# Filling up small constant tiles so that matmul operands in SBUF begin at multiples of 128 bytes

## The chip, the cores and the metric

The kernel runs on one core of one Trainium2 chip. The metric is the device time of one execution in microseconds (us). A lower number is better. The kernel of before was timed three times. Besides that there is one execution taken by the hardware profiler; the page and all rows below come from it.

## What is computed

Two batches of eight heads of attention (768 positions, head size 64), in which a query may only look at keys that belong to the same of 16 clusters, are followed by two layers that each expand 512 features to 2048 and go back to 512, without any routing. Everything is float32.

```python
# attention, per batch and head; q, k, v are 768 x 64
q_assign = argmax(normalised(q) @ normalised(centroids).T)     # 16 clusters
k_assign = argmax(normalised(k) @ normalised(centroids).T)
scores = where(q_assign == k_assign, q @ k.T / 8, -1e9)
x = softmax(scores) @ v                    # heads side by side: 1536 x 512
# layer 1                                  # layer 2
h = x @ w_in          # 512 -> 2048        h = x @ w_in
g = h * cos(h)                             g = h if h >= 1, 0 if h <= -1, else (h+1)**2/4
x = g @ w_out         # 2048 -> 512        out = g @ w_out
```

## The kernel before

**Precision.** TensorE multiplies in the type `F32R` (reduced float32). The kernel gets full precision by splitting a number into a high part (rounded to `F32R`) and a low part (the rest), and by adding products of the parts. So most operands exist twice: `th`/`tl` (transposed q and k), `phi`/`plo` (transposed probabilities), `xh`/`xl` (input of a layer), `gh`/`gl` (its hidden values), and the two halves of each weight tile `w_n`.

**Attention.** There are 8 pairs of heads (`prep_pair` prepares each) and 192 slots (`run_slot`), 24 for a pair. In one slot TensorE does three transposes of 128 columns (`p_transpose`, L527: the probabilities `p` are the operand that is loaded into the array, the identity `ident` is the one that is streamed), two score matmuls of 384 columns (`scores`, L475 and L478: one `st` tile is loaded, another is streamed) and two matmuls of 384 columns with v (`p_v`, L545 and L546: `vv` is loaded, `phi` and then `plo` are streamed). That is 192 x 4 = 768 matmuls of 384 columns in all. In some slots the preparation of the next pair comes on top (transposes L329, cluster products L367 and L368 that stream `cn`, transposes L449). ScalarE copies `phi` out of PSUM (L530) and takes the exponential (L493). VectorE makes `plo` (L535) and the row maximum `nm` (L484). GpSimd makes the parts of q, k, v and x.

**Layers.** For each of 2 layers, 4 quarters of the hidden features and 3 blocks of 512 tokens, `hidden` runs 48 matmuls of 512 columns and then `output` of the group before runs 48. Both go through `mm3` (L699 to L701). In `hidden` a weight is loaded and `xh`, `xl`, `xh` are streamed. In `output` of layer 1 a weight is loaded and `gh`, `gl`, `gh` are streamed; in layer 2 `gh` or `gl` is loaded and a weight is streamed. So 24 groups of 48 (1,152 matmuls) write `h` and 24 groups (1,152) write `y`. In the profile's rows a matmul's name gives its result first, then the streamed operand, then the loaded one, except that the identity of a transpose stands first as the streamed one.

**Where the tiles lie.** Each pool puts its tiles behind each other in a partition of SBUF and rounds a tile's size up to a multiple of 32 bytes. `cpool` holds the constants. In it a few tiles of 4 to 16 bytes take 32 bytes each, and what lies behind them begins at odd multiples of 32 bytes. In the attention's pool `css` (20 bytes) and the two `mx` tiles (96 bytes) do the same. Every piece of an operand that a matmul streams begins a multiple of 128 bytes behind the start of its tile; so the start of the tile decides.

What sets the order of work is the slot loop and, for most of the attention, a fixed order by hand; the change touches neither.

Of the kernel before, what the change touches and what calls it, by code (L numbers as in the profile page):

```python
# [8 lines left out]
F32 = mybir.dt.float32  # L9
F32R = mybir.dt.float32r  # L10
I32 = mybir.dt.int32
# [7 lines left out]
P = 128  # L19
# [13 lines left out]
def attention_moe_moe(  # L33
# [18 lines left out]
    nc = tc.nc  # L52
# [16 lines left out]
    cpool = ctx.enter_context(tc.tile_pool(name="cpool", bufs=1))  # L69
# [10 lines left out]
        nc.gpsimd.memset(ohbias[32 * r:32 * r + 32], 0.0 if is_q else -BIG)  # L80

    own = cpool.tile([P, 2, 2], F32, name="own")
    row = cpool.tile([P, 1], I32, name="row")
    nc.gpsimd.iota(row, pattern=[[0, 1]], base=0, channel_multiplier=1)
    nc.vector.tensor_scalar(row, row, C, None, ALU.bitwise_and)
    for h in range(2):
        half = BIG / C if h else -BIG / C
# [3 lines left out]
    idle = cpool.tile([P, 512], BF16, name="idle")  # L91
    nc.vector.memset(idle, 0.0)

    xh = cpool.tile([P, NPAIR, NT], F32R, name="xh")
    xl = cpool.tile([P, NPAIR, NT], F32R, name="xl")
    cn = cpool.tile([P, NPAIR, 2, 2, C], F32R, name="cn")
# [93 lines left out]
    with ExitStack() as actx:  # L190
        ap = actx.enter_context(tc.tile_pool(name="apool", bufs=1))
# [19 lines left out]
        def ins(x):  # L211
            return x.ins if hasattr(x, "ins") else x
# [20 lines left out]
        def centroid_setup(ct):  # L233
            sq = ct[:, 1]
            nc.vector.tensor_tensor(sq, ct[:, 0], ct[:, 0], ALU.mult)
            ss = ap.tile([P, 5], F32, tag="css", name="css")
            nc.vector.tensor_reduce(ss[:, 0:1], sq, AX.X, ALU.add)
            y = ss[:, 1:2]
            sq = nc.scalar.activation(y, ss[:, 0:1], AF.Sqrt)
            with tc.issue_after(ins(sq)):  # L240

                nc.scalar.activation(ss[:, 4:5], desc[:, 0:1], AF.Exp, scale=0.0)
            for _ in range(2):
                nc.vector.tensor_scalar(y, y, 1e-30, None, ALU.max)
                nc.vector.reciprocal(ss[:, 2:3], y)
                nc.vector.scalar_tensor_tensor(
                    ss[:, 3:4], ss[:, 0:1], ss[:, 2:3], y, ALU.mult, ALU.add)
                nc.vector.tensor_scalar(y, ss[:, 3:4], 0.5, None, ALU.mult)
            nc.vector.tensor_scalar(ss[:, 2:3], y, 1e-6, None, ALU.add)
            nc.vector.reciprocal(ss[:, 3:4], ss[:, 2:3])  # L250
            cd = ap.tile([P, HS], F32, tag="xt1", bufs=2, name="cd")[:, :P].rearrange(
                "p (r d) -> p r d", r=2)
            for r in range(2):
                nc.vector.tensor_scalar(cd[:, r], ct[:, 0], ss[:, 3:4], None, ALU.mult)
            nc.vector.memset(cn.bitcast(F32), 0.0)
            return cd
# [19 lines left out]
        def prep_pair(i):  # L276
# [95 lines left out]
                        yield  # L372

            G = NJ * 4
            mx = ap.tile([P, G], F32, tag="mx", bufs=2, name=f"mx{i}")
            eq = ap.tile([P, G, C], F32, tag="eq", bufs=1, name=f"eq{i}")
            if i == 0:
                run_idle(NIDLE[2], ins(mm))
# [217 lines left out]
        idle_o = ps_o.tile([P, 512], F32, tag="o", name="idle_o")  # L596
        run_idle(NIDLE[0])
        cd = centroid_setup(ct)
        for _ in prep_pair(0):
            next_slot()  # L600
# [9 lines left out]
        def run_slot(slot):  # L610
            g = slot + LEAD
            if slot in prep_at:
                preps.append(prep_pair(prep_at[slot]))
            if 0 <= slot < NSLOT:
                p_transpose(slot // NJ, slot % NJ)
            if 0 <= g < NSLOT:
                scores(g // 2, g % 2)
            for u, kt in pv_slots.get(slot, ()):
                p_v(u, kt)
            if slot % 2 == 0:  # L620
                for s in (slot - 1, slot):
                    if 0 <= s < NSLOT:
                        p_lo(s // NJ, s % NJ)
                if 2 <= g < NSLOT + 2:
                    row_exp(g // 2 - 1)
            next_slot()
            if slot == 60:
                issue_chunk(0)
            preps[:] = [p for p in preps if next(p, 0) != 0]
            if slot % 2 == 1 and 0 <= g < NSLOT:  # L630
                row_max(g // 2)
            if 64 <= slot < 192 and slot % 8 == 5:
                pump(1)
# [55 lines left out]
            parts(g, hi, lo)  # L689
        later(1, plus)  # L690

    mone = cpool.tile([P, 1], F32, name="mone")
    half = cpool.tile([P, 1], F32, name="half")
    nc.gpsimd.memset(mone, -1.0)
    nc.gpsimd.memset(half, 0.5)
    acc = [mp.tile([P, 4, 512], F32, tag=f"acc{blk}", name=f"acc{blk}") for blk in range(NB)]

    def mm3(o, lh, ll, rh, rl, first, last):
# [90 lines left out]
```

## Time and profile before

| | |
|---|---|
| three runs | 815.66, 816.03, 819.19 us; median 816.03 |
| profiled execution, span from its first to its last instruction | 818.6 us |
| TensorE matmul busy | 797.4 us, 97% of the span |
| VectorE busy | 629.7 us, 77% |
| ScalarE busy | 400.3 us, 49% |
| GpSimd busy | 282.6 us, 35% |
| attention, up to the first `h` matmul | 277.9 us |
| layers | the rest, 540.7 us |

The time that the profiled execution itself would have shown beside the three runs is not given; its span alone lies 2.6 us above their median. Matmuls are pipelined, so the duration of one (394 ns) is longer than the distance from its start to the start of the next (some 230 ns). For the pace of TensorE the starts are read, not the durations.

### The profile page before, as it was taken

What the parts mean: (1) busy time and instruction counts of PE and PEld (TensorE: products, weight loads), DVE (VectorE), ACT (ScalarE), POOL (GpSimd) and SP (SyncE); (2) the same over time, 40 slices, a digit from 0 to 9 for tenths busy, and PEclk for the clock granted to TensorE, in tenths of its full rate; (3) what the DMA queues carried; (4) which work ended last, traced back from release to release, by engine and by line L of the source; (5) the groups of instructions that cost most, each with busy time, mean ns of one, the idle gap of its engine ahead of it and who ended that gap; (6) DMA issues with size and microseconds to landing.
All of it is one profiled execution on the core that took longest, in us unless ns stands there. A gap on an engine that the chain in (4) does not pass through costs nothing.

```text
span 818.6 us, 11285 instructions
## 1 busy us (share of the span) xinstructions
PE 797.4 (97%) x4042; PEld 670.6 (82%) x4042; DVE 629.7 (77%) x957; ACT 400.3 (49%) x762; POOL 282.6 (35%) x425
## 2 busy tenths in 40 slices
PE   8899999999999999999999999999999999999998
PEld 5789988889888877888888888888888888888886
DVE  6878978968899787777977777898876987755552
ACT  3688878767788665443434333323444233222220
POOL 3347558574674532222221112332231122111110
PEclk9999999988999999999999999999999999999999
DMA  7875553565440103213121313112122221000012
GB/s 155 192 147 121 134 126 88 119 154 108 97 89 32 52 2 103 92 63 103 52 91 64 102 52 104 52 54 100 52 70 86 61 86 59 1 1 0 14 50 91
DMA packets 48183, 65.97 MB, mean 81 GB/s; under 512 B 27904, under 2 KB 32640, under 8 KB 48128
## 3 DMA queue, kind: packets, MB, share of 16 engines
q1 hardware_dynamic: 47984, 65.22, 29.5%
q8 instruction: 32, 0.52, 0.3%
q14 instruction: 23, 0.19, 0.1%
q10 hardware_dynamic: 144, 0.03, 0.0%
HBM read 43.02 MB, written 3.15 MB: 56 GB/s over the span
## 4 chain that ended last, share of the span: by engine, by line
PE 76%; DVE 10%; POOL 6%; ACT 4%; issue 2%; DMA 1%; SPq 0%; POOLq 0%; ACTq 0%; DVEq 0%
PE y L699 11%; PE y L700 11%; PE y L701 11%; PE h L701 10%; PE h L699 10%; PE h L700 10%; PE pt L527 4%; DVE plo L535 3%; DVE nm L484 3%; PE s L475 2%; PE s L478 2%; PE o L546 2%; PE o L545 2%; ACT phi L530 1%; PE pd L368 1%
## 5 line engine op out<-in xcount | busy, mean ns | idle before, releaser
L657 POOL TENSOR_SCALAR gh<-g 128x512 fp32r<-128x512 f32 x96 | 71.5, 745 | 278.0 <-DVE g L688 157.4
L699 PE MATMUL h<-xh,w 128*128 128x512 f32 x384 | 151.4, 394 | 0.5 <-DVE g L674 0.5
L700 PE MATMUL h<-xl,w 128*128 128x512 f32 x384 | 151.4, 394 | 0.0
L701 PE MATMUL h<-xh,w 128*128 128x512 f32 x384 | 151.3, 394 | 0.0
L535 DVE TENSOR_TENSOR plo<-pt,phi 128x384 fp32r<-128x384 f32 x192 | 99.6, 547 | 16.6 <-ACT phi L530 15.8
L530 ACT ACTIVATE phi<-pt 128x384 fp32r<-128x384 f32 x192 | 93.2, 494 | 36.2 <-PE pt L527 34.4
L484 DVE TENSOR_REDUCE nm<-s 128x1 f32<-128x768 f32 x96 | 91.0, 948 | 19.8 <-PE s L478 18.8
L527 PE MATMUL pt<-ident,p 128*128 128x128 f32 x576 | 98.5, 279 | 7.8 <-DVE plo L535 5.8
L684 ACT ACTIVATE p<-h,mone 128x512 f32<-128x512 f32 x48 | 33.1, 690 | 130.0 <-DVE m L683 129.6
L493 ACT ACTIVATE p<-s,nm 128x768 f32<-128x768 f32 x96 | 86.6, 902 | 8.8 <-DVE nm L484 7.8
L661 DVE TENSOR_TENSOR gl<-g,gh 128x512 fp32r<-128x512 f32 x96 | 71.6, 746 | 20.0 <-POOL gh L657 15.3
L699 PEld LDWEIGHTS h<-xh,w 128*128 128x128 f32 x384 | 71.9, 187 | 18.4 <-DVE g L674 1.0
L701 PEld LDWEIGHTS h<-xh,w 128*128 128x128 f32 x384 | 71.8, 187 | 17.7
L527 PEld LDWEIGHTS pt<-ident,p 128*128 128x128 f32 x576 | 69.9, 141 | 20.0 <-issue 4.2
L700 PEld LDWEIGHTS h<-xl,w 128*128 128x128 f32 x384 | 71.9, 187 | 17.5
L475 PE MATMUL s<-st,st 128*128 128x384 f32 x192 | 81.6, 425 | 2.5 <-ACT p L493 2.3
L139 ACT ACTIVATE wx<-wraw 128x1024 f32<-128x1024 f32 x32 | 36.5, 1140 | 95.5 <-DMA wraw<-in_moe_w_out_dram 47.7
L699 PE MATMUL y<-gh,w 128*128 128x512 f32 x192 | 74.9, 390 | 1.3 <-POOL w L155 1.3
L700 PE MATMUL y<-gl,w 128*128 128x512 f32 x192 | 74.8, 390 | 0.0
L700 PE MATMUL y<-w,gh 128*128 128x512 f32 x192 | 74.8, 390 | 0.0
L699 PE MATMUL y<-w,gh 128*128 128x512 f32 x192 | 74.7, 389 | 0.0
L738 DVE TENSOR_TENSOR acc<-y,acc 128x512 f32<-128x512 f32 x72 | 49.2, 685 | 33.1 <-PE y L701 33.1
(120 smaller groups left out, 1636.3 us busy)
## 6 DMA issues: line engine op xcount, KB each, us to landing
wraw<-in_moe_w_in_dram SPq DMA_DIRECT2D x16, 1024.0 KB, 5.1
wraw<-in_moe_w_out_dram SPq DMA_DIRECT2D x16, 1024.0 KB, 4.9
st<-t SPq DMA_DIRECT2D x24, 192.0 KB, 4.3
st<-th SPq DMA_DIRECT2D x9, 384.0 KB, 4.0
st<-tl SPq DMA_DIRECT2D x18, 192.0 KB, 4.0
st<-th SPq DMA_DIRECT2D x18, 192.0 KB, 4.3
nat<-in_q_dram SPq DMA_DIRECT2D x8, 384.0 KB, 5.1
nat<-in_k_dram SPq DMA_DIRECT2D x8, 384.0 KB, 5.8
```

The source lines that it names most:

```text
L475: nc.tensor.matmul(s[:, step, :HS], qt[:, 0, cols], kt[:, 0, kc], start=True, stop=False)
L484: nc.vector.tensor_reduce(nm, s[:, :, :HS], AX.XY, ALU.max, negate=True)
L493: nc.scalar.activation(p, s[:, :, :HS], AF.Exp, bias=nm, accum_out=dens[u][:, jj, 0:1])
L527: nc.tensor.transpose(ps[:, jj * P:(jj + 1) * P], p[:, kt * P:(kt + 1) * P], ident)
L530: nc.scalar.activation(hi, ps, AF.Copy)
L535: nc.vector.tensor_tensor(lo, ps, hi.bitcast(F32), ALU.subtract)
L657: nc.gpsimd.tensor_scalar(hi, g, 1.0, 0.0, ALU.mult, ALU.add)
L661: nc.vector.tensor_tensor(lo, g, hi.bitcast(F32), ALU.subtract)
L699: nc.tensor.matmul(o, lh, rh, start=first, stop=False)
L700: nc.tensor.matmul(o, lh, rl, start=False, stop=False)
L701: nc.tensor.matmul(o, ll, rh, start=False, stop=last)
L738: nc.vector.tensor_tensor(a, po, a, ALU.add)
```

## The change

Four small tiles get more columns, of which only the first ones are used, and the two one-column constants `mone` and `half` become columns of one 128-byte tile `ones`, which is placed before `xh`.

```diff
-    row = cpool.tile([P, 1], I32, name="row")
+    row = cpool.tile([P, 24], I32, name="row")[:, 0:1]
...
     idle = cpool.tile([P, 512], BF16, name="idle")
     nc.vector.memset(idle, 0.0)
 
+    ones = cpool.tile([P, 32], F32, name="ones")
+    mone, half = ones[:, 0:1], ones[:, 1:2]
+    nc.gpsimd.memset(mone, -1.0)
+    nc.gpsimd.memset(half, 0.5)
     xh = cpool.tile([P, NPAIR, NT], F32R, name="xh")
...
-            ss = ap.tile([P, 5], F32, tag="css", name="css")
+            ss = ap.tile([P, 32], F32, tag="css", name="css")
...
-            mx = ap.tile([P, G], F32, tag="mx", bufs=2, name=f"mx{i}")
+            mx = ap.tile([P, 32], F32, tag="mx", bufs=2, name=f"mx{i}")[:, :G]
...
-    mone = cpool.tile([P, 1], F32, name="mone")
-    half = cpool.tile([P, 1], F32, name="half")
-    nc.gpsimd.memset(mone, -1.0)
-    nc.gpsimd.memset(half, 0.5)
```

The instructions of all engines, their shapes, their order and their waits stay the same, row for row; only addresses change. The start of each tile, as a remainder by 128 bytes, in the two built programs:

| tiles | part in the matmuls | before | after |
|---|---|---|---|
| `xh`, `xl` | streamed, `h` (512 columns) | 64 | 0 |
| `cn` | streamed, cluster products (64 columns) | 64 | 0 |
| `idle` | both operands of filler matmuls at the start (bf16) | 64 | 0 |
| `st` | streamed and loaded, scores (384 columns) | 32 | 0 |
| `phi`, `plo` | streamed, with v (384 columns) | 96 | 0 |
| `vv`, `p`, `rb` | loaded | 96 | 0 |
| `th`, `tl`, `dots` | loaded | 32 | 0 |
| `eq`, `natv`, `oht`, `t32`, most `xt` | none | 32 or 96 | 0 |
| `w_n`, `gh`, `gl`, `ident`, `nat`, `wraw`, `acc`, `g`, `r`, `n` | streamed or loaded, or none | 0 | 0 |

## Rows read from the trace of the kernel before

**Rows 1.** The page: busy us, share and instructions of each engine; chain's shares

```profile
PE 797.4 (97%) x4042; PEld 670.6 (82%) x4042; DVE 629.7 (77%) x957; ACT 400.3 (49%) x762; POOL 282.6 (35%) x425
...
PE 76%; DVE 10%; POOL 6%; ACT 4%; issue 2%; DMA 1%; SPq 0%; POOLq 0%; ACTq 0%; DVEq 0%
```

**Rows 2.** Busy time by stretches: length, engines (instructions), PEclk, DMA share, GB/s

```profile
core 0: us, PE busy (x) PEld busy (x) DVE busy (x) ACT busy (x) POOL busy (x), PEclk, DMA share, GB/s
...
59.00:105.50 46.50, 45.88 (x317) 42.73 (x316) 40.34 (x75) 38.55 (x89) 32.67 (x53) 1.00 0.53 125
...
178.90:189.10 10.20, 10.20 (x42) 10.10 (x41) 5.16 (x11) 3.73 (x8) 1.93 (x4) 0.50 1.09 261
...
226.00:277.80 51.80, 48.59 (x321) 44.56 (x321) 49.03 (x87) 42.97 (x96) 28.13 (x47) 1.00 0.20 48
...
305.00:560.00 255.00, 253.74 (x1103) 206.29 (x1102) 205.27 (x268) 103.15 (x162) 63.24 (x72) 1.00 0.24 79
560.00:792.00 232.00, 232.00 (x1009) 188.72 (x1008) 162.60 (x218) 72.57 (x110) 45.08 (x58) 1.00 0.14 46
```

**Rows 3.** The chain that ended last, by line, share of the span

```profile
by line: PE y L699 10.6%; PE y L700 10.6%; PE y L701 10.6%; PE h L701 10.1%; PE h L699 10.1%; PE h L700 10.1%; PE pt L527 4.0%; DVE plo L535 3.3%; DVE nm L484 2.6%; issue 2.3%; PE s L475 1.9%; PE s L478 1.7%; PE o L546 1.5%; PE o L545 1.5%;
```

**Rows 4.** Timeline of PE, first rows of groups of 48: start us, duration us

```profile
395.24 0.39 PE L699 MATMUL y<-gh,w 128*128 128x512 f32 x1
...
406.14 0.39 PE L699 MATMUL h<-xh,w 128*128 128x512 f32 x1
406.38 0.39 PE L700 MATMUL h<-xl,w 128*128 128x512 f32 x1
...
417.34 0.39 PE L699 MATMUL y<-gh,w 128*128 128x512 f32 x1
...
693.44 0.39 PE L699 MATMUL h<-xh,w 128*128 128x512 f32 x1
...
704.64 0.39 PE L699 MATMUL y<-w,gh 128*128 128x512 f32 x1
...
715.54 0.39 PE L699 MATMUL h<-xh,w 128*128 128x512 f32 x1
```

**Rows 5.** Timeline of PE in the attention, from L478 to the next slot's transposes

```profile
202.72 0.34 PE L478 MATMUL s<-st,st 80*128 80x384 f32 x1
202.90 0.34 PE L545 MATMUL o<-phi,vv 128*128 128x384 f32 x1
203.08 0.34 PE L546 MATMUL o<-plo,vv 128*128 128x384 f32 x1
203.25 0.49 PE L527 MATMUL pt<-ident,p 128*128 128x128 f32 x3
```

**Rows 6.** Groups by line: count, busy us, mean ns, idle before and who ended it

```profile
L527 PEld LDWEIGHTS pt<-ident,p 128*128 128x128 f32 x576 | 69.9, 141 | 20.0 <-issue 4.2 <-PE s L478 3.8 <-PE r L577 2.8
...
L329 PEld LDWEIGHTS ptq<-ident,nat 128*128 128x128 f32 x96 | 11.4, 141 | 4.8 <-ACT t L337 1.2 <-issue 1.2 <-DVE tl L296 0.7
...
L535 DVE TENSOR_TENSOR plo<-pt,phi 128x384 fp32r<-128x384 f32 x192 | 99.6, 547 | 16.6 <-ACT phi L530 15.8
...
L738 DVE TENSOR_TENSOR acc<-y,acc 128x512 f32<-128x512 f32 x72 | 49.2, 685 | 33.1 <-PE y L701 33.1
```

**Rows 7.** Waits from 26 to 278 us: engine, line, waited for, total us, times, longest

```profile
ACT phi L530 <- PE pt L527: 33.4, 51, 2.6
...
PEld pd L367 <- ACT t L337: 3.0, 5, 0.9
```

**Rows 8.** Timeline of PE before and in the only long stretch at the lower clock

```profile
172.02 0.34 PE L546 MATMUL o<-plo,vv 128*128 128x384 f32 x1
173.06 0.55 PE L329 MATMUL ptq<-ident,nat 128*128 128x128 f32 x3 [0.70 <-ACT t L337]
...
180.08 0.52 PE L546 MATMUL o<-plo,vv 128*128 128x384 f32 x1
180.40 0.52 PE L545 MATMUL o<-phi,vv 128*128 128x384 f32 x1
```

## The prediction

> **What bounds the kernel now.** I read the page's engine line first: TensorE is busy 97% of the span and no other engine above 77% [rows 1]. That share is an average, so I split the span into stretches. From 305 to 792 us, in the layers, TensorE has no idle time to speak of (253.74 of 255.00 us, then 232.00 of 232.00), while VectorE, the next engine, is at 205.27 and 162.60 us, that is 80% and 70% [rows 2]. There the time is the pace of the matmuls. In the attention it is less clear. TensorE is at 45.88 of 46.50 us from 59 to 105.5, but from 226 to 277.8 VectorE is ahead of it (49.03 of 51.80 against 48.59) [rows 2]. The chain of waits says the same: TensorE holds 76% of it, the two kinds of layer matmuls alone 62%, and the rest is shared by all four engines [rows 1, 3].
>
> Since a matmul's duration overlaps the next one, I take the pace from starts. A group of 48 `h` matmuls takes 417.34 - 406.14 = 11.20 us in layer 1 and 704.64 - 693.44 = 11.20 us in layer 2. A group of 48 `y` matmuls takes 406.14 - 395.24 = 10.90 and 715.54 - 704.64 = 10.90 us [rows 4]. So `h` runs at 233.3 ns a matmul and `y` at 227.1, although both have 512 columns, the same shapes and the same kind of instruction, and this in both layers. What differs is the streamed operand: `xh` and `xl` begin at 64 by 128 bytes, while `gh`, `gl` (layer 1) and `w` (layer 2) begin at 0. The loaded operand does not explain it: it is an aligned weight in `h` and in `y` of layer 1. Other work beside it does not explain it well either, as the second `h` row after a switch already starts 0.24 us behind the first [rows 4], when nothing of that group is computed yet. This comparison within one kernel is my main evidence.
>
> **The change part by part.** No instruction is added, removed or moved, and no wait changes; the two constant fills on GpSimd keep their place. So every term is a change of the duration or the pace of what is there already.
>
> *`xh` and `xl` from 64 to 0.* There are 24 groups of `h`. If they go at the pace of `y`, each saves 11.20 - 10.90 = 0.30 us, 24 x 0.30 = 7.2 us. All of it lies where TensorE is without gaps and the next engine has 20% room [rows 2], so I book it in full. Bounds: 0, if the difference has another cause, and 7.2.
>
> By the Trainium skill ("TensorE: Matmul & The Clock Gate", section "Back-to-back issue gap") a warm matmul of N columns takes N/2.4 + 2.5 ns, an estimate of 215.8 ns for 512, with no term for where the operand begins. Both paces here are above it, and they differ from each other, so the rows decide against it.
>
> *Streamed `st`, `phi` and `plo` from 32 and 96 to 0.* One slot shows their pace: from L478 to the next slot's transposes three matmuls take 203.25 - 202.72 = 0.53 us, 177 ns each [rows 5]. None of these 768 matmuls is aligned now, so the aligned pace has to come from `y`: 227.1 x 384/512 = 170.3 ns, an estimate. The saving is 6.7 ns each, 768 x 6.7 = 5.1 us of TensorE's time. Bounds: 0 and 5.1. Not all of it reaches the end. The chain holds 1.9 + 1.7 + 1.5 + 1.5 = 6.6% of 818.6 us on these four lines, 54 us [rows 3], and 54/0.177 is 305 of the 768 matmuls. I take 305 x 6.7 = 2.0 us. Of the other 3.1 us nothing arrives, since other engines hold the chain there: VectorE's `plo` and row maximum `nm` have 5.9% of it [rows 3], and they are what is late next.
>
> *Loaded operands (`vv`, `p`, `st`, `th`, `tl`).* The 576 loads of `p` at 96 take 141 ns in the mean, and the 96 loads of `nat`, at 0 already, take 141 too [rows 6]. I book nothing.
>
> *VectorE, ScalarE, GpSimd.* `plo` (384 elements, at 96) takes 547 ns on VectorE and `acc` (512 elements, at 0) 685 ns [rows 6]. The difference is 138 ns for 128 elements; three times that is 414, which leaves a fixed part of 133 ns. There is no sign of a cost at 96. I book zero, and zero for the two other engines by this nearest row. A cost of a few ns that this pair cannot show would matter most on VectorE: 5 ns for each of the 192 `plo` is 1 us, to either side.
>
> *Transfers.* The copies into `st` and the loads of `natv` get other addresses too. The chain holds 1% of transfers [rows 1], 8 us; a tenth of that to either side would be 0.8 us. I book zero. *`cn`* is streamed in 192 short matmuls; at the 6.2 ns that part `h` from `y` it would be 1.2 us at most, and its lines are too small to be listed in the chain [rows 3]: zero, with 1.2 us as the bound. `idle` serves fillers at the start: zero.
>
> The sum is 7.2 + 2.0 = 9.2 us. Against the profiled span that gives 818.6 - 9.2 = 809.4. That execution is not a typical one: from 178.9 to 189.1 us TensorE was granted 0.50 of its clock (1.2 GHz, the lower of its two levels) [rows 2], and L546 and L545 start 0.32 us apart instead of the 0.18 of the slot above [rows 5, 8]. A stretch of 10.2 us at half pace costs at most 5.1 us, and the span is 2.6 us above the median of the runs, so I think that the faster runs were spared it. I apply the gain to the median: 816.0 - 9.2 = 806.8.
>
> **The rivals.**
>
> *Nothing changes (816.0).* Then the start of a tile does not matter, and `h` is slower for another reason that stays, for instance something that goes with its PSUM tiles. For it: no row shows the same operand at two starts, so alignment is inferred from different tiles. The Trainium skill speaks for it ("SBUF — State Buffer", section "Specifications (TRN2)"): it gives lines of 16 bytes, and starts at 32, 64 and 96 are multiples of that, so by it nothing is gained. Against it: the paces of `h` and `y` in both layers [rows 4], and the slot's 177 ns, which per column (0.461 ns) is nearer to `h` (0.456) than to `y` (0.444) [rows 4, 5].
>
> *The layers gain, the attention gives its part back (808.8).* The 7.2 us come, and in the attention another engine takes TensorE's place at once. For it: VectorE at 95% from 226 to 277.8 us [rows 2]. Against it: TensorE at 99% from 59 to 105.5 us [rows 2], and 51 waits of ScalarE for the transposes, 33.4 us [rows 7], which end sooner when TensorE is ahead. 816.0 - 7.2 = 808.8.
>
> *Slower, by the clock (822).* The stretch at 0.50 came some us after TensorE had sat waiting for ScalarE's copy of q and k, 1.04 us from 172.02 to 173.06 [rows 8]. Faster matmuls make such waits longer. There are 5 more for `t` before the cluster products [rows 7]. Each further stretch costs up to 5.1 us: two would eat the gain, and three give 816.0 - 9.2 + 3 x 5.1 = 822.1. Against it: only one stretch came here from all these waits, and the saving is 27 ns in a slot of over 1,000.
>
> That the change does not do what it says is out: the starts in the built program are at 0, as the table shows.
>
> **How the numbers follow.** The forecast, with the layers' 7.2 us and some of the attention's, gets 0.60; the layers alone 0.22; nothing 0.13; slower 0.03; and 0.02 is for more than the whole 12.3 us, should loads or transfers gain too. The range: with all of the attention's 5.1 us the time is 816.0 - 12.3 = 803.7, and the bounds of transfers (0.8) and `cn` (1.2) give 801.7. At the upper end the layers alone give 808.8, and half of a stretch at the lower clock on top gives 811.4. From 801.7 to 811.4 about 0.18 is left out, the case of nothing above all. Half a per cent, about what a measurement of this kernel tells from no change, is 4.1 us. Faster by over 0.5% means below 811.9: 0.60 + 0.22 + 0.02 = 0.84. Within it: 0.13. Slower: 0.03.
>
> **What would show it.** In the timeline after, the starts of 48 `h` matmuls should take 10.90 us, and those of `y` still 10.90; if `h` stays at 11.20, the first term and its reason fall. In a slot the three intervals behind L478 should shrink from 0.53 to 0.51 us. The means of VectorE's, ScalarE's and GpSimd's groups should stay within some ns. The first `h` matmul should come some 2 us earlier, if both executions have as much time at the lower clock. If the attention becomes shorter by 5 us, I have undervalued its part; if it does not, TensorE's waits for ScalarE and VectorE there should have grown by what the matmuls gave. The prediction is wrong as a whole if the start matters only for one kind of matmul, or if the clock falls more often.

## The result and the profile after

The changed kernel takes 808.96 us (median of 4 runs, 807.92 to 812.58), the kernel before 817.61 (4 runs now, 815.66 to 821.18). The ratio is 0.9888, with a 95% interval from 0.9853 to 0.9924. So the change makes the kernel 0.8 to 1.5% faster. The forecast of 806.8 us was 2.2 us too low; the time lies in its range. A later set on one chip, with 5 runs of the changed kernel, gave 809.0 against 816.42, 0.9903 (0.9886 to 0.9921). Some executions hold 10 us at the lower clock in the attention and are some 3.5 us longer for it; the profiled one of before is such an execution and that of after, the fastest of its four, is not, so the spans (818.6 and 806.1 us) differ by more than the kernels do.

The page of after has the same instructions and nearly the same shares:

```profile
span 806.1 us, 11285 instructions
...
PE 785.0 (97%) x4042; PEld 666.4 (83%) x4042; DVE 629.0 (78%) x957; ACT 399.7 (50%) x762; POOL 281.6 (35%) x425
```

TensorE is busy 12.4 us less than in [rows 1]; the other engines are within 1 us of what they were. The timeline of PE with the first rows of groups of 48, the counterpart of [rows 4]:

```profile
388.95 0.39 PE L699 MATMUL y<-gh,w 128*128 128x512 f32 x1
...
399.83 0.39 PE L699 MATMUL h<-xh,w 128*128 128x512 f32 x1
...
410.71 0.39 PE L699 MATMUL y<-gh,w 128*128 128x512 f32 x1
...
693.61 0.39 PE L699 MATMUL y<-w,gh 128*128 128x512 f32 x1
...
704.49 0.39 PE L699 MATMUL h<-xh,w 128*128 128x512 f32 x1
...
715.37 0.39 PE L699 MATMUL y<-w,gh 128*128 128x512 f32 x1
```

All four groups take 10.88 us: 410.71 - 399.83 and 715.37 - 704.49 for `h`, 399.83 - 388.95 and 704.49 - 693.61 for `y`. Before, `h` took 11.20. `y` gained 0.02 as well: before, its first five matmuls behind an `h` group were some 231 ns apart, and now they are 226 to 227 apart like the others.

One slot of the attention, the counterpart of [rows 5]:

```profile
197.87 0.34 PE L482 MATMUL s<-st,st 80*128 80x384 f32 x1
198.05 0.34 PE L549 MATMUL o<-phi,vv 128*128 128x384 f32 x1
198.22 0.34 PE L550 MATMUL o<-plo,vv 128*128 128x384 f32 x1
198.40 0.49 PE L531 MATMUL pt<-ident,p 128*128 128x128 f32 x3
```

The three intervals are 198.40 - 197.87 = 0.53 us, as before. The matmuls of 384 columns have gained nothing.

Busy time by stretches of after, to be read beside [rows 2]:

```profile
178.20:188.50 10.30, 10.12 (x70) 9.41 (x69) 8.49 (x16) 7.31 (x16) 3.55 (x7) 1.00 1.03 267
221.00:272.90 51.90, 48.72 (x321) 44.63 (x321) 49.15 (x87) 43.05 (x96) 28.12 (x47) 1.00 0.18 48
300.00:555.00 255.00, 253.40 (x1118) 209.58 (x1117) 207.12 (x270) 103.38 (x162) 63.12 (x72) 1.00 0.23 79
555.00:787.00 232.00, 232.00 (x1026) 192.01 (x1025) 165.24 (x223) 73.87 (x111) 46.16 (x60) 1.00 0.14 47
```

In the layers TensorE gets through 1,118 matmuls in 255 us instead of 1,103, and VectorE goes from 205.27 to 207.12 us busy in that time: it has room. The last 321 matmuls of the attention take as long as they did (51.90 us from 221.0, 51.80 before).

Where the 12.5 us between the two spans come from is seen in four places of PE's timeline. First of before (start of the slots; two marks around the stretch at the lower clock; first `h`):

```profile
25.61 0.55 PE L527 MATMUL pt<-ident,p 128*128 128x128 f32 x3
...
171.16 0.49 PE L527 MATMUL pt<-ident,p 128*128 128x128 f32 x3
...
193.42 0.38 PE L527 MATMUL pt<-ident,p 128*128 128x128 f32 x2
...
277.86 0.39 PE L699 MATMUL h<-xh,w 128*128 128x512 f32 x1
```

The same marks of after:

```profile
25.15 0.55 PE L531 MATMUL pt<-ident,p 128*128 128x128 f32 x3
...
170.52 0.49 PE L531 MATMUL pt<-ident,p 128*128 128x128 f32 x3
...
188.57 0.38 PE L531 MATMUL pt<-ident,p 128*128 128x128 f32 x2
...
272.92 0.39 PE L699 MATMUL h<-xh,w 128*128 128x512 f32 x1
```

Up to the slots 0.5 us are gone. Between the two middle marks lie 12 slots, which took 22.26 us and take 18.05; these 4.2 us are the lower clock and no work of the change. The rest of the attention gives 0.3 us. From the first `h` to the end it is 818.6 - 277.86 = 540.7 against 806.1 - 272.92 = 533.2 us: 7.5 us, and that is the work of the change.

The paces alone would have given more: 24 x 0.32 us for `h` and 23 x 0.02 for the `y` groups behind an `h` group are 8.1 us. Some 0.6 us went into longer waits at the start of the layers. The waits of TensorE there, before and after (total us, times, longest us):

```profile
PE y L699 <- POOL w L155: 1.3, 1, 1.3
PE h L699 <- DVE g L674: 0.5, 1, 0.5
...
PE y L699 <- POOL w L159: 1.6, 1, 1.6
PE h L699 <- DVE g L678: 0.8, 1, 0.8
```

That trace shows the gain at its best. Six more kernels below have `h` at 10.88 us (layers only, all at 64, attention apart, the whole change again, the matmuls by themselves and the sweep). In the trace of each, TensorE waits in layer 2 for ScalarE's `p`, which reads `h` out of PSUM, 0.5 to 0.9 us in all (1.3 in the matmuls by themselves). In no trace with a slower `h`, and not in that of after, is there such a wait. In the whole change again it is this one:

```profile
583.17 0.50 PE L699 MATMUL h<-xh,w 128*128 128x512 f32 x1 [0.61 <-ACT p L688]
```

Its layers take 534.1 us. In five of the six they take 534.1 to 534.7 us, so there the layers gained 6.0 to 6.7 us and not 7.5.

### The profile page after: what moved, and what is told of

The parts are those of the page before. It is cut to its first block, busy times and chain, and to the rows that moved or that the text cites. A ratio compares the mean times of both kernels' runs of the same rounds, so it can differ in the third digit from the quotient of the medians.

```text
span 806.1 us, 11285 instructions
## 1 busy us (share of the span) xinstructions
PE 785.0 (97%) x4042; PEld 666.4 (83%) x4042; DVE 629.0 (78%) x957; ACT 399.7 (50%) x762; POOL 281.6 (35%) x425
## 4 chain that ended last, share of the span: by engine, by line
PE 77%; DVE 9%; POOL 7%; ACT 4%; issue 2%; POOLq 0%; DVEq 0%; ACTq 0%
PE y L699 11%; PE y L701 11%; PE y L700 11%; PE h L699 10%; PE h L701 10%; PE h L700 10%; PE pt L531 4%; DVE plo L539 3%; DVE nm L488 2%; PE s L479 2%; PE s L482 2%; PE o L550 2%; PE o L549 2%; PE idle_o L222 1%; ACT phi L534 1%
## 5 line engine op out<-in xcount | busy, mean ns | idle before, releaser
L699 PE MATMUL h<-xh,w 128*128 128x512 f32 x384 | 149.5, 389 | 0.8 <-DVE g L678 0.8
L700 PE MATMUL h<-xl,w 128*128 128x512 f32 x384 | 149.5, 389 | 0.0
L701 PE MATMUL h<-xh,w 128*128 128x512 f32 x384 | 149.4, 389 | 0.0
L688 ACT ACTIVATE p<-h,ones 128x512 f32<-128x512 f32 x48 | 33.0, 688 | 125.7 <-DVE m L687 125.3
L701 PE MATMUL y<-w,gl 128*128 128x512 f32 x192 | 74.7, 389 | 0.0
```

The source lines that it names most:

```text
L699: nc.tensor.matmul(o, lh, rh, start=first, stop=False)
L700: nc.tensor.matmul(o, lh, rl, start=False, stop=False)
L701: nc.tensor.matmul(o, ll, rh, start=False, stop=last)
```

## The experiments

All kernels keep the instructions, their order and the data of the changed kernel (attention only: of the kernel before); they move tiles, and two of them add matmuls of their own at the start. All at 64, x at 0, the two kernels with `xh` apart from `xl`, the matmuls by themselves and the sweep were run once each; there the paces in the trace decide, not the time.

### Which half of the change works

The changed kernel with its two fills in the attention undone (**layers only**), and the kernel before with these two alone (**attention only**):

```diff
# layers only, against the changed kernel
-            ss = ap.tile([P, 32], F32, tag="css", name="css")
+            ss = ap.tile([P, 5], F32, tag="css", name="css")
...
-            mx = ap.tile([P, 32], F32, tag="mx", bufs=2, name=f"mx{i}")[:, :G]
+            mx = ap.tile([P, G], F32, tag="mx", bufs=2, name=f"mx{i}")
# attention only: the same two lines the other way round, in the kernel before
```

> The changed kernel with the fills of css and mx undone: the operands of the layers (xh, xl, weights, gh, gl) begin at 0, those of the attention at 32 and 96 as before. Theory A (all of the gain is the pace of the h matmuls, and the start of an operand does nothing in the attention): 48 h matmuls take 10.88 us, the slots keep 177 ns a matmul of 384 columns, and the time is that of the whole change, some 7 us under the kernel before. The prediction's theory (the attention gives 2.0 us more): the time is 2 us above that of the whole change, some 5 us under the kernel before.

> The kernel before with css and mx filled up alone: the operands of the attention begin at 0, xh, xl and cn at 64 as before. Theory A: 48 h matmuls take 11.20 us, nothing else changes, and the time is that of the kernel before within 1 us. The prediction's theory: 2.0 us faster than before, with the three intervals behind the second score matmul at 0.51 us instead of 0.53.

Layers only: 808.81 us (5 runs), ratio 0.9889 (0.9866 to 0.9913), which is the whole change. Attention only: 817.09 us (12 runs) beside 817.38, ratio 0.9997 (0.9978 to 1.0016). The prediction's 2.0 us for the attention are not there; theory A holds. The fills of `css` and `mx` are worth nothing that can be measured.

### Is it the start, or the pair?

In the attention each streamed operand and its loaded partner had the same remainder by 128 bytes (32 and 32, 96 and 96), while in `h` it was 64 against 0. So a rival to "the start counts" was "the pair counts". Two kernels put 64 bytes in front of `xh` (**all at 64**) or behind `cn` (**x at 0, the rest at 64**).

```diff
# all at 64
+    cpool.tile([P, 16], F32, name="pad0")
     xh = cpool.tile([P, NPAIR, NT], F32R, name="xh")
# x at 0, the rest at 64
     cn = cpool.tile([P, NPAIR, 2, 2, C], F32R, name="cn")
+    cpool.tile([P, 16], F32, name="pad0")
```

> The changed kernel with 64 bytes more in front of xh, so that xh, xl, cn, the weights, gh, gl and all operands of the attention except the identity begin at 64. Theory of the start (a streamed operand that does not begin at 0 costs 6 ns in a matmul of 512 columns, whatever is loaded): 48 h matmuls take 11.20 us and 48 y matmuls 11.20 us too, some 14 us more in all than the changed kernel (24 + 24 groups at 0.30 us). Theory of the pair (it costs only when the streamed and the loaded operand begin at different remainders, as xh at 64 against a weight at 0 did, while the attention's pairs 32/32 and 96/96 agreed): both kinds of groups take 10.88 us, and the time is that of the changed kernel within its spread.

> The changed kernel with 64 bytes more behind cn: xh, xl and cn begin at 0, the weights, gh, gl and all operands of the attention except the identity at 64. Theory of the start: 48 h matmuls (x at 0 is streamed) take 10.88 us, 48 y matmuls (gh, gl or a weight at 64 is streamed) 11.20 us. Theory of the pair: 48 h matmuls (x at 0 against a weight at 64) take 11.20 us, 48 y matmuls (64 against 64) 10.88 us. Both give some 7 us more than the changed kernel, so the groups decide and not the time.

PE's timeline with everything at 64:

```profile
388.94 0.39 PE L700 MATMUL y<-gh,w 128*128 128x512 f32 x1
...
399.82 0.39 PE L700 MATMUL h<-xh,w 128*128 128x512 f32 x1
...
410.70 0.39 PE L700 MATMUL y<-gh,w 128*128 128x512 f32 x1
```

With x at 0 and the rest at 64:

```profile
390.59 0.39 PE L700 MATMUL y<-gh,w 128*128 128x512 f32 x1
...
401.49 0.39 PE L700 MATMUL h<-xh,w 128*128 128x512 f32 x1
...
412.69 0.39 PE L700 MATMUL y<-gh,w 128*128 128x512 f32 x1
```

With no operand of the layers at a multiple of 128, both kinds of groups take 10.88 us, and the time is 809.45 us. With `xh` and `xl` at 0, exactly as in the changed kernel, `h` takes 11.20 us again because the weights have moved, and the time is 815.74. The start of the streamed operand alone decides nothing. The pair counts.

### How much of a difference, and whose

> The changed kernel with xh at 32 and xl at 96 by 128 bytes and everything else at 0, the weights too. Theory of the pair in its widest form (any difference by 128 between the streamed and the loaded operand costs): 48 h matmuls take 11.20 us or more, with the two rows that stream xh (difference 32) and the one that streams xl (difference 96) some 233 ns apart from the next start. Theory of the pair for a difference of 64 alone: 10.88 us, 227 ns throughout. 48 y matmuls take 10.88 us by both.

> The changed kernel with xh at 64 and everything else at 0, xl too. Of three h matmuls two stream xh and one streams xl. If the cost belongs to the matmul that streams the operand at another remainder: two of three distances are 233 ns and the one behind the xl matmul 227, so 48 take 11.09 us (32 x 6.5 ns over 10.88). If any difference in the stream of matmuls slows them all: 11.20 us. If the extra time needs both operands off: 10.88.

The pads are like those above, 32 and 64 bytes in front of `xh` and `xl` in the first kernel, 64 in front of each in the second; in the first 32 more follow behind `xl`. In both they add up to 128 bytes, so that the weights stay at 0 by 128. With `xh` at 32 and `xl` at 96 a group of `h` takes 11.27 us, with `xh` at 64 alone 11.24. So differences other than 64 cost as well. One streamed operand out of line also slows matmuls that stream the other one: in the second kernel the distances from start to start go 226, 235, 239, 234, 236, 237 ns and round again, and the 239 and one 237 are behind matmuls that stream `xl`, which lies at 0 like the weights. (The second kernel's time of 821.05 us holds the stretch at the lower clock, from 178.4 to 188.7 us; its groups are outside of it. The first took 816.74.)

### The attention's pairs put apart

Here `st` of k lies 64 bytes off `st` of q, and `phi` and `plo` lie 64 bytes from `vv` by 128.

```diff
+                if n == 1 and i == 0 and h == 0:
+                    ap.tile([P, 16], F32, tag="pad_st", name="pad_st")
...
+            if u == 0 and kt == 0:
+                ap.tile([P, 16], F32, tag="pad_phi", name="pad_phi")
             hi = ap.tile([P, HS], F32R, tag="phi", bufs=6, name=f"phi{u}_{kt}")
```

> The changed kernel with the operands of the attention put apart: st of q at 0 against st of k at 64, vv and p at 64 against phi and plo at 0; the layers stay at 0. Theory of the pair: the matmuls of 384 columns now cost what the h matmuls cost before, 6 ns each or three quarters of that: 177 ns become 181 to 183, 768 x 4.7 to 6.2 = 3.6 to 4.8 us of TensorE's time, of which, by the share that these matmuls have of the chain (305 of 768), 1.4 to 1.9 us reach the end. If matmuls of 384 columns are limited by something else, or the operands' starts matter only at 512 columns: 177 ns stay, and the time is that of the changed kernel within 0.5 us.

> The changed kernel as it is, for a closer time beside the others of this set and to see how many of its executions have the 10 us at the lower clock in the attention. If the change has no part in that stretch, about as many as of the kernel before (some half of its runs lie 3.5 us above the rest). If it has one, clearly fewer. Runs without it: 808 to 809 us against 815.5 to 816.5.

Apart: 809.3 us (6 runs), ratio 0.9909 (0.9891 to 0.9927). The whole change again: 809.0 us (5 runs, 808.56 to 809.14), ratio 0.9903 (0.9886 to 0.9921). None of its 5 runs lies 3 us above the others, against 3 of 11 of the kernel before beside it; with so few runs that does not show that the change has a part in the stretch at the lower clock. The slot apart:

```profile
197.95 0.34 PE L485 MATMUL s<-st,st 80*128 80x384 f32 x1
198.13 0.34 PE L554 MATMUL o<-phi,vv 128*128 128x384 f32 x1
198.31 0.34 PE L555 MATMUL o<-plo,vv 128*128 128x384 f32 x1
198.49 0.49 PE L534 MATMUL pt<-ident,p 128*128 128x128 f32 x3
```

The three intervals are 0.54 us instead of 0.53, and 0.3 us in the time is no difference that these runs tell. The theory of the pair, carried over to 384 columns at full price, missed: it had expected 1.4 to 1.9 us. The sweep below shows that the two places tried here were not the dear ones.

### The matmuls by themselves

The changed kernel with extra matmuls at its start, from a tile of constants, once with the streamed operand at its start (alike) and once 64 bytes further on (apart):

```diff
+        def alike(n):
+            nc.tensor.matmul(idle_o[:, :n], mw[:, :P], mb[:, :n], start=True, stop=True)
...
+        def apart(n):
+            nc.tensor.matmul(idle_o[:, :n], mw[:, :P], mb[:, 16:16 + n], start=True, stop=True)
```

> The changed kernel with extra matmuls ahead of its own work, whose results are not used: after 40 fillers, 24 matmuls of 512 columns from a tile at 0 with a loaded operand at 0 (alike) and 24 from the same tile 64 bytes further on (apart), then the same with 384, 256 and 128 columns, then 12 rounds of three transposes and four matmuls of 384 columns, alike, and 12 apart. If the cost belongs to any matmul whose operands are apart: apart is slower by 6 to 7 ns at 512 columns and by a like amount at 384 and 256, and a round of the last kind is slower by 20 to 28 ns. If it depends on the number of columns: 6 to 7 ns at 512 and nothing at 384. If it depends on a long run of equal matmuls: slower at 384 in the run of 24 and equal in the rounds with transposes, which is what the attention showed. At 128 columns the load is the longer part: no difference. The time is some 60 us more by the extra work.

PE's timeline, L608 alike and L611 apart; the duration of a row is that of 24 matmuls:

```profile
17.13 5.67 PE L611 MATMUL idle_o<-mb,mw 128*128 128x512 f32 x24
22.64 4.33 PE L608 MATMUL idle_o<-mb,mw 128*128 128x384 f32 x24
26.80 4.32 PE L611 MATMUL idle_o<-mb,mw 128*128 128x384 f32 x24
30.96 3.04 PE L608 MATMUL idle_o<-mb,mw 128*128 128x256 f32 x24
33.83 2.99 PE L611 MATMUL idle_o<-mb,mw 128*128 128x256 f32 x24
36.66 2.79 PE L608 MATMUL idle_o<-mb,mw 128*128 128x128 f32 x24
```

At 384 columns both take (26.80 - 22.64)/24 = 173.3 ns, at 256 apart is even a little faster (118 against 120), at 128 both are some 111 ns apart. The cluster products with 64 columns are 111 ns apart too (median, before and after), so there the columns do not set the pace; I take it to be the load. The rounds of three transposes and four matmuls take 1.03 us either way. At 512 columns alike settles at 226.7 ns (its last 12 distances; the first matmuls still ran at the lower clock), but apart at 229 and not at 233. So at this point the number of columns mattered, and 64 bytes in this direction cost a third of what 64 bytes cost in the layers. The loaded tile here lies 256 bytes by 512 from the streamed one, and that did no harm.

### cn alone, x alone

```diff
# cn at 64
+    cpool.tile([P, 16], F32, name="pad0")
     cn = cpool.tile([P, NPAIR, 2, 2, C], F32R, name="cn")
+    cpool.tile([P, 16], F32, name="pad1")
# x at 64: pad0 in front of xh, pad1 in front of cn
```

> The changed kernel with cn alone at 64. It asks whether the stretch of 10 us at the lower clock, seen in about 4 of 10 executions of the kernel before and in 1 of 20 of the kernels with x, cn and the fillers' tile at 0, goes with cn. If it does: some executions 3.5 us above the others. If not: all at 808 to 810 us. The pace of h stays at 10.88 us for 48 either way.

> The changed kernel with xh and xl at 64, cn and all others at 0: the first term of the prediction undone alone. 48 h matmuls take 11.20 us, the time is 7.2 to 7.7 us above the changed kernel, 815.5 to 816.5 us. If the stretch at the lower clock goes with the place of x, some executions lie 3.5 us above that; if it goes with cn or the fillers' tile, none does.

The second came as expected: 11.20 us for 48 `h`, 815.68 us (12 runs), ratio 0.9996 (0.9982 to 1.0011); the first term of the prediction, undone alone, takes the whole gain away. The first did not. With x, the weights, `gh` and `gl` all at 0 by 128, it took 815.41 us (12 runs), ratio 0.9992 (0.9981 to 1.0004), and its timeline shows why:

```profile
402.63 0.40 PE L701 MATMUL h<-xh,w 128*128 128x512 f32 x1
...
413.82 0.39 PE L701 MATMUL y<-gh,w 128*128 128x512 f32 x1
```

`h` is at 11.19 us although everything is at a multiple of 128. The two pads moved the weights by 128 bytes and left x in place. So agreement by 128 is not enough either. The starts in the built programs, as the distance of the streamed from the loaded operand of `h` by 256 bytes, put all kernels in order, since the loaded pieces, too, begin a multiple of 256 bytes behind the start of their tile:

| kernel | distance by 256 | 48 `h`, us |
|---|---|---|
| before; attention only | 192 | 11.20 |
| after; layers only; attention apart | 0 | 10.88 |
| all at 64 | 0 | 10.88 |
| x at 0, the rest at 64 | 192 | 11.20 |
| `xh` at 32, `xl` at 96 | 160, 224 | 11.27 |
| `xh` at 64 | 192, 0 (`xl`) | 11.24 |
| `cn` at 64 | 128 | 11.19 |
| x at 64 | 192 | 11.20 |

As to the stretch at the lower clock, both kernels had 1 execution of 12 that lay 3 us or more above the others, and the kernel before beside them 2 of 23. Neither `cn` nor x was shown to have a part in it. There is a shorter stretch as well: the profiled executions of `cn` at 64 (143.2 to 146.6 us) and of attention only (177.8 to 181.2 us) have 3.4 us at a granted clock of 0.50, and their attention takes 249.2 us from the first transposes to the first `h`, where that of after takes 247.8.

### The sweep

```diff
+        def even(n, m):
+            nc.tensor.matmul(idle_o[:, :n], mw, mb[:, 8 * m:8 * m + n], start=True, stop=True)
... (odd is the same)
+        for n, times in ((512, 48), (384, 24)):
+            for m in range(16):
+                for _ in range(times):
+                    (odd if m % 2 else even)(n, m)
...
+            if n == 0:
+                ap.tile([P, 32], F32, tag="pad_p", name="pad_p")
             p = ap.tile([P, 2, HS], F32, tag="p", bufs=P_BUFS, name=f"p{n}")
```

> The changed kernel with extra matmuls ahead of its own work, whose results are not used: after 40 fillers, 16 runs of 48 matmuls of 512 columns, the streamed operand beginning 0, 32, 64, ... 480 bytes further on in each run while the loaded operand stays at 0 by 512, then the same 16 places with 24 matmuls of 384 columns each. Besides, p, phi and plo lie 128 bytes further on, so that in the attention all streamed and loaded operands agree by 256 bytes. The theory after cn alone at 64 put all weights 128 bytes from x and made h slow again: what counts is the distance between the streamed and the loaded operand by 256 bytes. It expects 226.7 ns at 0 and at 256, 233 ns at 128, 192 and 448 (the distances that were slow in the layers), about 229 at 64 and 320, and the second half of the 16 like the first. If the distance counts by 512: 256 is unlike 0, although the matmuls alone at a distance of 256 ran at 226.7. If it counts by 128 after all: 0, 128, 256 and 384 all at 226.7. At 384 columns: 173 to 175 ns at every place. For the attention: if its matmuls with v paid for p, phi and plo lying 128 bytes from vv, they come down from 175 to 178 ns to some 172; if not, nothing moves. The time is some 250 us more by the extra work.

PE's timeline; each row is a run of 48, the streamed operand 32 bytes further on in each; the pace is the distance of the starts of two rows by 48:

```profile
22.28 11.37 PE L613 MATMUL idle_o<-mb,mw 128*128 128x512 f32 x48
33.49 11.16 PE L610 MATMUL idle_o<-mb,mw 128*128 128x512 f32 x48
44.48 11.37 PE L613 MATMUL idle_o<-mb,mw 128*128 128x512 f32 x48
55.70 11.36 PE L610 MATMUL idle_o<-mb,mw 128*128 128x512 f32 x48
66.89 11.40 PE L613 MATMUL idle_o<-mb,mw 128*128 128x512 f32 x48
78.14 11.35 PE L610 MATMUL idle_o<-mb,mw 128*128 128x512 f32 x48
89.33 11.35 PE L613 MATMUL idle_o<-mb,mw 128*128 128x512 f32 x48
100.52 11.05 PE L610 MATMUL idle_o<-mb,mw 128*128 128x512 f32 x48
111.40 11.37 PE L613 MATMUL idle_o<-mb,mw 128*128 128x512 f32 x48
122.61 11.16 PE L610 MATMUL idle_o<-mb,mw 128*128 128x512 f32 x48
...
197.99 4.33 PE L610 MATMUL idle_o<-mb,mw 128*128 128x384 f32 x24
202.15 4.40 PE L613 MATMUL idle_o<-mb,mw 128*128 128x384 f32 x24
206.39 4.39 PE L610 MATMUL idle_o<-mb,mw 128*128 128x384 f32 x24
```

Distances of 32, 64, 96, 128, 160, 192 and 224 bytes give 233.5, 229.0, 233.8, 233.1, 234.4, 233.1 and 233.1 ns. 256 gives (111.40 - 100.52)/48 = 226.7, as does the run at 0 once its first ten matmuls are over. From 288 on the numbers repeat to 0.2 ns in all seven rows that follow. So the distance counts by 256 bytes, 0 is the best place, 64 a middling one, and the rest cost 6.4 to 7.7 ns. At 512 columns this is what the theory expected, at every place that it named.

At 384 columns the theory expected 173 to 175 ns everywhere, and that missed by a little. Places 0, 32 and 64 settle at 173.3 ns ((202.15 - 197.99)/24 at 64), but 96, 128 and 160 take some 176 to 176.7 ((206.39 - 202.15)/24 at 96), 192 and 224 some 174.5, and the second eight places repeat this. So the distance counts at 384 columns too, with other good places and about half the cost. The kernel with the attention's pairs put apart had `st` at a distance of 64 and `phi` and `plo` at 192, which cost 0 and about 1.4 ns here: it could not show much.

The pad in front of `p` brought `phi` and `plo` from a distance of 128 by 256 to `vv`, which they had before and after the change, to 0; `st` against `st` was at 0 all along. The matmuls with v did not get faster: from the `phi` matmul to the `plo` matmul it is 178 ns in the median, after the change 175. The attention took as long as after the change, 247.8 us from the first transposes to the first `h` in both. So in the slots the places did not show in the time, and no version was found that is better than the changed kernel; layers only is its equal with fewer edits.

## Why the prediction came out as it did

- **The main evidence held.** The comparison of `h` and `y` within the kernel before [rows 4] gave 0.30 us for a group. It came as 0.32 (11.20 to 10.88), and in the profiled execution the layers got 7.5 us shorter, where 7.2 were booked. That is 8.1 us by the paces (the first matmuls of `y` behind `h` gained too) less some 0.6 in longer waits.
- **Booked in full, and nearly so.** VectorE had the room that [rows 2] showed. But "without gaps" was an average over long stretches: a faster `h` lengthened two waits at the start of the layers and, in the other traces of kernels with the same `h`, brought in a new one for ScalarE, which is busy only 103.38 of the 255 us. In five of those traces the layers gained 6.0 to 6.7 us, less than the 7.2.
- **The reason was wrong, though the number was nearly right.** "What differs is the streamed operand" was true, but "begins at 64 by 128" was the wrong way to say it: what counts is its distance from the loaded operand, by 256 bytes. The step that failed is the exclusion of the loaded operand. I had compared its start in `h` and in `y`, found it the same, and dropped it, when it was half of the pair. The change works because its fills, as they add up, bring x and the weights to a distance of 0. That they do was luck, as nothing in the change asked for it. Had they put the weights 128 bytes further on, as in the kernel with `cn` at 64, the description of the change would have been met in every word with no gain.
- **The attention's 2.0 us did not come.** The term was wrong twice. Its size was scaled from `y` by columns, 170.3 ns; the sweep has no place below 173.3, so at most 3 to 4 ns a matmul were there to gain, not 6.7. And the change did not touch the pairs: by 256, `st` against `st` stayed at 0 and `phi`, `plo` against `vv` stayed at 128. The slot's 177 ns, read as nearer to `h` than to `y`, proved nothing, since the pace is not proportional to the columns: with good places it is 226.7 ns for 512, 173.3 for 384 and 120 for 256, that is some 53 ns for every 128 columns and a fixed 13 ns (worked out from these three). Scaling by 384/512 shrank the fixed part as well, by the 3 ns that 170.3 is too low. Nor did the 177 hold for all 768: from a first score matmul (L475) to the second it is 259 ns in the median, before and after.
- **The rivals.** "The layers gain, the attention gives its part back" was the nearest in time (808.8; measured 808.96), with a chance of 0.22, while the favoured case with 0.60 did not come. It came for another reason than the one given: no other engine took the place of TensorE in the attention, its matmuls were not faster. "Nothing changes" and "slower, by the clock" did not come. (The wait that the latter started from was read too long: its row gives 0.70 us of idle time; 1.04 us is from start to start.) The dismissal of "the change does not do what it says" stood on the table of starts by 128; it should have asked by what size a start is to be read.
- **The zeros** for loads, VectorE, ScalarE, GpSimd and `cn` held: `plo` takes 549 ns (547 before), `phi` 493 (494), GpSimd's `gh` 743 (745), the loads of `p` 140 (141), and the cluster products stay 111 ns apart. The zero for transfers was not looked at by itself.
- **The median.** The forecast was set against 816.0, the median of three runs. More runs put the kernel before at 815.4 to 816.4 without a stretch at the lower clock in the attention, so the shift away from the profiled span was needed.

## What to carry to other kernels

When two groups of equal matmuls in one kernel run at different paces, compare the places of both operands of each pair in SBUF, not only of the one that differs in name. For long runs of `F32R` matmuls with 512 columns, let the streamed and the loaded tile begin at the same place by 256 bytes; pad sizes to multiples of 256, so that a small constant added later does not move one of them alone. Do not scale a pace from one number of columns to another: measure it. Here runs of 24 to 48 matmuls at the start of the kernel were enough, with the first ten left out. And when the busiest engine gets faster, look in several executions for waits that were not there before.

## What the runs showed of the hardware

- The pace of 128x512 `F32R` matmuls at the full clock is 226.7 ns when the streamed and the loaded operand lie 0 or 256 bytes apart, 229 at 64 and 320, and 233 to 234 at the other multiples of 32. With 384 columns it is 173.3 to 176.7, with the slow places at 96 to 160; with 256 columns it is 118 to 120.
- The slowing does not stay with the matmul whose operands are out of line: with one of two streamed operands out of line five of six distances are 234 to 239 ns instead of 227. Behind a switch from slow to fast pairs some matmuls are still slow: the first five or six of a `y` group before the change (226 to 236 ns), but only the first one (233 ns) in the sweep.
- By the Trainium skill ("TensorE: Matmul & The Clock Gate", section "Step-by-step: what each phase is for") loading the next weights does not take read bandwidth from the running matmul. The sweep sets a limit to that: the pace depends on how the two operands lie to each other, 226.7 against 233 to 234 ns with nothing else changed. By what mechanism, and which of the two reads waits, no run here shows.
- What brings the 10 us at the lower clock into some executions of the attention is open. Judged by the time, 2 of 23 executions of the kernel before had it in one set and 8 of 17 in another.
